# Query tiles of consecutive rows, sines in one run and paired scale factors in a fused attention and convolution kernel

## The chip, the cores and the metric

The kernel runs on one core of one Trainium2 chip. The metric is the time of one execution on the device in microseconds (us); quoted times are medians, with the lowest and highest in brackets. Engines: PE multiplies matrices (PEld is its weight load), DVE is the vector engine, ACT the scalar engine, POOL issues most loads, SP issues stores. In these traces the instructions of an engine start in the order in which they were compiled, and a ready one behind a waiting one waits with it, so the compiled order on each engine matters. Times inside a run are counted from the start of its span; line numbers with an L are those of the kernel named, and the changed kernel's differ from the kernel before.

## The reference, cut to what matters

Eight batches, eight heads, 576 rows, 64 columns per head. Attention with random features is followed by a gated convolution along the rows.

```python
h = x @ omega.T - ...;  phi = exp(h - max(h)) / sqrt(m)      # features of q and k
kv = einsum('bhsm,bhsd->bhmd', phi(k), v);  z = sum(phi(k))
num, den = phi(q) @ kv, phi(q) @ z
x = (num / (den + 1e-06)).transpose(0, 2, 1, 3).reshape(B, S, H * D)
x1, x2, x3 = split(x @ w_proj)
y = x1 * irfft(rfft(x2) * rfft(filter)) * x3
out = y @ w_out
```

## The kernel before

Two generators are woven into one stream of instructions: `attention()` works on pairs of batches, `hyena()` does the projections and the convolution of the pair before. Each `yield` says how much of the work it just put out weighs, and the weaver takes turns by these weights.

A query tile holds, in each partition, four consecutive rows of every head (packets of 512 B in the load):

```python
t_ = nat.tile([P, H, NT, D], BF16, name=f"{which}n", bufs=2)
nc.gpsimd.dma_start(
    out=t_[:, hs].rearrange("p h t d -> p h (t d)"),
    in_=src[b, hs, 0:SM, :].rearrange("h (p t) d -> p h (t d)", t=NT))
```

The values are scaled by one factor per row of each head, which one broadcast element carries:

```python
vc = att.tile([P, H, NT, D + 1], BF16, name="vc", bufs=2)
...
nc.vector.tensor_tensor(out=vc[:, :, :, 0:D], in0=vn[:],
    in1=vc[:, :, :, D : D + 1].to_broadcast([P, H, NT, D]), op=ALU.mult)
```

The output of a batch is normalised into four tiles `xb`, then turned back behind all four, with a permutation and a strided write:

```python
for t in range(NT):
    ps = two_banks()
    for h in range(H): ...                     # 8 matmuls with kv
    xbs.append(normalise(ps))
    yield 3 * U
for cb in range(CB):
    tp = bank()
    for t in (3, 0, 1, 2):
        nc.tensor.matmul(out=tp[:].rearrange("p (c t) -> p t c", t=NT)[:, t],
                         lhsT=xbs[t][:, cb, :], rhs=perm[:], start=True, stop=True)
    nc.scalar.copy(out=xt[:, :, cb, :], in_=tp[:].rearrange("p (g c) -> p g c", g=4))
    yield U
```

The loads stand at the head of the program: keys, values and queries of batch 0, the three thirds of `wproj`, keys, queries and values of batch 1, left-over queries, `wout`, keys and queries of batch 2, then the filter. `load_filter()` also puts out seven additions and subtractions on DVE, the "folds", as soon as the weave reaches it. Sines for the transform tables are computed in three runs on ACT with exponentials between them.

The softmax here doesn't subtract the row's maximum and nothing guards it: scores larger than these inputs give would overflow.

Of the kernel before, what the change touches and what calls it, by code (L numbers as in the profile page):

```python
# [18 lines left out]
P = 128  # L19
# [23 lines left out]
def kernel(  # L43
# [14 lines left out]
    DM = 512  # L58
# [30 lines left out]
    def load_main(b, which, parts=1, between=None):  # L89
        src = {"q": q, "k": k, "v": v}[which]  # L90
        t_ = nat.tile([P, H, NT, D], BF16, name=f"{which}n", bufs=2)
        step = H // parts
        for h0 in range(0, H, step):
            hs = slice(h0, h0 + step)
            nc.gpsimd.dma_start(
                out=t_[:, hs].rearrange("p h t d -> p h (t d)"),
                in_=src[b, hs, 0:SM, :].rearrange("h (p t) d -> p h (t d)", t=NT),
            )
            if between is not None and h0 == 0:
                between()  # L100
        nat_tiles[which, b] = t_
# [27 lines left out]
    load_main(0, "q", 2)  # L129

    wproj = const.tile([P, CB, 3 * DM], BF16, name="wproj")
    for g in (1, 0, 2):
        cs = slice(g * DM, (g + 1) * DM)
        nc.gpsimd.dma_start(
            out=wproj[:, :, cs], in_=moe_w_proj[:, cs].rearrange("(c p) n -> p c n", p=P)
        )
    for w in "kqv":
        load_main(1, w)
# [12 lines left out]
    for j in range(2):  # L151
# [5 lines left out]
    perm = const.tile([P, P], BF16, name="perm")  # L157
    id48 = ident[:, 0:96].rearrange("p (j q) -> p j q", j=2)
    nc.vector.tensor_copy(
        out=perm[:, 0:64].rearrange("p (j q) -> p j q", j=2), in_=id48[:, :, 0:32]  # L160
    )
    nc.vector.tensor_copy(out=perm[:, 64:96], in_=ident[:, 96:128])
    nc.vector.tensor_copy(
        out=perm[:, 96:128].rearrange("p (j q) -> p j q", j=2), in_=id48[:, :, 32:48]
    )


# [3 lines left out]
    for j in range(NV):  # L171
        t_ = const.tile([P, 2, H, D + 1], BF16, name=f"vcl{j}")
        nc.vector.memset(t_[:], 0.0)
        vcl_buf.append(t_)
# [26 lines left out]
    def sines():  # L201
# [48 lines left out]
        def sine(bias, o, x):  # L250
            nc.scalar.activation(out=o, in_=x, func=AF.Sin, scale=-two_pi / S, bias=bias)

        def periodic(bias, o, r_):

            sine(
                bias,
                o[:, 0 : 3 * P].rearrange("p (j c) -> p j c", j=3),
                r_[:, 0:P].unsqueeze(1).to_broadcast([P, 3, P]),
            )
            sine(  # L260
                bias,
                o[:, 3 * P : S].rearrange("p (j s) -> p j s", j=3),
                r_[:, P : P + SL].unsqueeze(1).to_broadcast([P, 3, SL]),
            )


        gn = hy.tile([P, S], BF16, name="x2", bufs=2)
        for n, pieces in (
# [29 lines left out]
            if c == 0:  # L298
                sine(ph[:, 2:3], gtab[:, 0, :], ra)
                sine(zb[:], gtab[:, 1, :], r)  # L300
            elif c == 1:
                sine(ph[:, 0:1], gtab[:, 2, :], ra)
            else:
                periodic(ph[:, 1:2], gtab[:, 3], ra[:, 0:192])
                periodic(ph[:, 0:1], gn[:], ra[:, 192:384])
        for j in range(2):
            ts(out=gns[:, j], in0=gn[:], scalar1=mk[:, j : j + 1], scalar2=None, op0=ALU.mult)
        nc.vector.memset(fwar[:], 0.0)

# [37 lines left out]
    sines()  # L347
# [7 lines left out]
    def load_filter():  # L355
        ff = hy.tile([P, 4, DM], BF16, name="x13", bufs=3)
        fg = hy.tile([P, 4, DM], BF16, name="x13", bufs=3)
        fh = hy.tile([P, 4, DM], BF16, name="x13", bufs=3)
        fsrc = moe_filter_fft.rearrange("(j s) n -> s j n", j=3)
        nc.gpsimd.dma_start(out=ff[:, 0:3], in_=fsrc[0:P])  # L360
        for j in range(2):
            rows = slice(j * SL, (j + 1) * SL)
            nc.gpsimd.dma_start(out=fg[rows, 0], in_=fsrc[P:192, j])
            nc.gpsimd.dma_start(out=fg[rows, 1], in_=fsrc[P:192, 2])
            nc.gpsimd.dma_start(out=fh[rows, 0:3], in_=fsrc[P:192])
        for x, o, y, z, op in (
            (ff, 3, 0, 1, ALU.add),
            (ff, 3, 3, 2, ALU.add),
            (ff, 0, 0, 2, ALU.subtract),
            (ff, 1, 1, 2, ALU.subtract),  # L370
            (fg, 0, 0, 1, ALU.subtract),
            (fh, 0, 0, 1, ALU.add),
            (fh, 0, 0, 2, ALU.add),
        ):
            nc.vector.tensor_tensor(out=x[:, o], in0=x[:, y], in1=x[:, z], op=op)
        filt["b"] = [ff[:, 0], ff[:, 1], fg[:, 0]]
        filt["a"] = [ff[:, 3], fh[:, 0]]
# [56 lines left out]
    def max_to_c(c_out, ekf, n):  # L434
# [13 lines left out]
        with nc.allow_low_precision(reason="a bf16 factor of both sums"):  # L448
            for o, part in c_out:
                m_ = mx[part, 0:n]  # L450
                if n > H:
                    m_ = m_.rearrange("p (h t) -> p h t", h=H)
                nc.vector.reciprocal(out=o, in_=m_)
# [15 lines left out]
    def normalise(ps):  # L469
# [4 lines left out]
        xb = att.tile([P, CB, P], BF16, name="xb", bufs=4)  # L474
# [8 lines left out]
        return xb  # L483

    def attention():
        U = 1.0 / 90.0
        for i in range(B // 2):
# [5 lines left out]
            for bb in range(2):  # L493
# [5 lines left out]

                kt = att.tile([P, H, 2, P], BF16, name="kt", bufs=1)  # L500
                qt = att.tile([P, H, 2, P], BF16, name="qt", bufs=1)

                def turn(dst, src, g):
                    transposes(
                        dst[:, 4 * g : 4 * g + 4, :, :].rearrange("p h u c -> p (h u) c"),
                        [
                            src[:, h, 2 * u2 : 2 * u2 + 2, :].rearrange("p t d -> p (t d)")
                            for h in range(4 * g, 4 * g + 4)
                            for u2 in range(2)
                        ],  # L510
# [12 lines left out]
                for g in range(2):  # L523
                    turn(kt, kn, g)
                    yield 3 * U
                    for h in (4 * g, 4 * g + 2):
                        key_features(
                            ek[:, h : h + 2, :, :].rearrange("p h t m -> p (h t m)"),
                            [kt[:, hh, u2, :] for hh in (h, h + 1) for u2 in range(2)],
                        )  # L530
                        yield 3 * U
                if bb == 0:
# [12 lines left out]
                        [(vcl[hs, j, :, D], hs) for j, hs in enumerate(halves)], ekl[:], H  # L545
                    )
                    for j, hs in enumerate(halves):
                        nc.vector.tensor_tensor(
                            out=vcl[hs, j, :, 0:D],
                            in0=vl[hs, :, :],  # L550
                            in1=vcl[hs, j, :, D : D + 1].to_broadcast([SL, H, D]),
                            op=ALU.mult,
                        )
                    yield U
                for g in range(2):
                    turn(qt, qn, g)
                    yield 3 * U

                if bb == 1:
# [18 lines left out]
                vc = att.tile([P, H, NT, D + 1], BF16, name="vc", bufs=2)  # L578
                max_to_c(
                    [(vc[:, :, :, D], slice(0, P))],  # L580
# [3 lines left out]
                nc.vector.tensor_tensor(  # L584
                    out=vc[:, :, :, 0:D],
                    in0=vn[:],
                    in1=vc[:, :, :, D : D + 1].to_broadcast([P, H, NT, D]),
                    op=ALU.mult,
                )

                eqt = att.tile([P, NPAIR, 2, 2, 2, P], BF16, name="eqt", bufs=1)
                for pr in range(NPAIR):
                    ps = two_banks()
                    for j in range(2):
# [3 lines left out]
                            rhs=qt[:, 2 * pr : 2 * pr + 2, :, :],  # L598
# [3 lines left out]
                    nc.scalar.activation(  # L602
                        out=eqt[:, pr].rearrange("p j h u c -> p j (h u c)"), in_=ps[:], func=AF.Exp
                    )
                    yield 3 * U

                ps = two_banks()
                for h in range(H):
                    o = ps[:, h // 4, (h % 4) * (D + 1) : (h % 4 + 1) * (D + 1)]
                    nc.tensor.matmul(  # L610
                        out=o, lhsT=ekl[:, h, :], rhs=vcl[:, bb, h, :], start=True, stop=False
                    )
                    for t in range(NT):
# [3 lines left out]
                            rhs=vc[:, h, t, :],  # L617
# [13 lines left out]
                for t in range(NT):  # L631
                    ps = two_banks()
                    for h in range(H):
                        nc.tensor.matmul(
                            out=ps[:, h // 4, (h % 4) * (D + 1) : (h % 4 + 1) * (D + 1)],
                            lhsT=eqt[:, h // 2, t % 2, h % 2, t // 2, :],
# [6 lines left out]

                for cb in range(CB):
                    tp = bank()
                    for t in (3, 0, 1, 2):
                        nc.tensor.matmul(  # L647
                            out=tp[:].rearrange("p (c t) -> p t c", t=NT)[:, t],
                            lhsT=xbs[t][:, cb, :],
                            rhs=perm[:],  # L650
                            start=True,
                            stop=True,
                        )
                    nc.scalar.copy(  # L654
                        out=xt[:, :, cb, :], in_=tp[:].rearrange("p (g c) -> p g c", g=4)
                    )
                    yield U
# [13 lines left out]
            tp = bank()  # L671
            for cb in range(CB):
                nc.tensor.matmul(
                    out=tp[:, cb * P : (cb + 1) * P],
                    lhsT=xb[:, cb, :],
                    rhs=ident[:],
                    start=True,
                    stop=True,
                )
            nc.scalar.copy(out=xtl[:], in_=tp[:].rearrange("p (c j s) -> p j c s", c=CB, j=2))  # L680
# [275 lines left out]
```

## Time and profile before

| | before |
|---|---|
| time, us | 365.05 (364.85 to 365.65), 3 runs |
| span of the profiled run, us | 363.8 |
| busy PE, DVE, ACT, POOL, us | 303.5, 227.8, 198.2, 47.5 |
| values of batch 0 / 1 scaled at | 41.3 / 64.2 |
| left-over product x13l of pair 0 / 1 / 2 / 3 at | 140.8 / 233.5 / 291.8 / 341.3 |

`vc` of a batch is the last thing that kv of that batch needs; x13l ends the projections of a pair of batches; xt, used further down, is a batch's output after the turn back. From x13l of pair 0 to that of pair 2 two pairs pass in the settled part of the kernel; I call these 150.9 us the steady stretch. The lines of the profile are in the prediction.

### The profile page before, as it was taken

Reading aid. Unit: us, or ns where it says so; the run is one execution under the profiler, and the core shown is the slowest. Engines: PE = TensorE matmul, PEld = TensorE weight load, DVE = VectorE, ACT = ScalarE, POOL = GpSimd, SP = SyncE. Lnnn points to the kernel's source line nnn. Section 1 sums busy time; section 2 is a strip of 40 time slices with the busy share of each in tenths; the row PEclk is TensorE's granted clock in tenths of the full one; section 3 lists DMA queues with packets and bytes.
Section 4 is the critical chain, followed back from the end, with each engine's and each line's share of the span. In section 5 each row is a group of like instructions: output and inputs, shape, how many; then the busy total and the mean of one; then the engine's idle time right before and its main releaser. Section 6 shows DMA issues by size and latency. Waiting matters only on the chain.

```text
span 363.8 us, 6044 instructions
## 1 busy us (share of the span) xinstructions
PE 303.5 (83%) x2434; PEld 175.6 (48%) x2434; DVE 227.8 (63%) x460; ACT 198.2 (54%) x302; POOL 47.5 (13%) x70
## 2 busy tenths in 40 slices
PE   1715386897678999988999996999998999988993
PEld 1503373753245557546556545756443544433541
DVE  7438679641976787697289999386069343076440
ACT  2796138089954654733886761664583322763123
POOL 8723352200110100213000000000000000000000
PEclk9966689899586999999999999999999999999998
DMA  8999997921674241789941100003401014220034
GB/s 89 185 202 196 185 136 88 155 28 12 69 114 55 14 53 20 142 108 169 165 54 37 29 0 2 2 17 100 146 23 36 2 59 141 63 58 2 0 117 144
DMA packets 47740, 29.26 MB, mean 80 GB/s; under 512 B 14432, under 2 KB 42080, under 8 KB 47712
## 3 DMA queue, kind: packets, MB, share of 16 engines
q0 software_dynamic: 40912, 17.31, 39.5%
q1 hardware_dynamic: 6800, 11.57, 10.5%
q8 instruction: 19, 0.31, 0.4%
q14 instruction: 9, 0.07, 0.1%
HBM read 34.64 MB, written 9.44 MB: 121 GB/s over the span
## 4 chain that ended last, share of the span: by engine, by line
PE 46%; DVE 23%; DMA 13%; ACT 11%; issue 5%; POOL 1%; POOLq 0%; ACTq 0%; DVEq 0%
PE h L837 9%; PE h L882 7%; PE h L899 7%; PE h L715 6%; DMA x<-in_moe_filter_fft_dram 5%; DMA kn<-in_k_dram 4%; DVE xb L475 4%; PE h L647 3%; DVE vc L584 3%; DMA vn<-in_v_dram 2%; PE a L614 2%; PE h L853 2%; ACT ek L467 2%; DMA qn<-in_q_dram 2%; PE h L878 2%
## 5 line engine op out<-in xcount | busy, mean ns | idle before, releaser
L837 PE MATMUL h<-xt,wproj 128*128 128x512 bf16 x256 | 61.0, 387 | 3.4 <-DVE x L846 3.4
L467 ACT ACTIVATE ek<-a 128x1024 bf16<-128x1024 f32 x32 | 32.4, 1044 | 36.7 <-PE a L460 36.7
L909 ACT COPY osb<-h 128x512 f32<-128x512 f32 x36 | 21.1, 586 | 44.2 <-PE h L899 34.9
L837 PEld LDWEIGHTS <-wproj 128*128 128x128 bf16 x256 | 25.2, 100 | 32.7 <-issue 6.4
L845 ACT CAST x<-h 128x512 bf16<-128x512 f32 x32 | 19.2, 600 | 28.8 <-PE h L837 21.9
L602 ACT ACTIVATE eqt<-a 128x1024 bf16<-128x1024 f32 x32 | 32.2, 1065 | 4.2 <-PE a L595 4.1
L889 DVE TENSOR_TENSOR yt<-x,h 128x512 bf16<-128x512 bf16 x32 | 21.9, 684 | 18.3 <-PE h L882 18.3
L846 DVE TENSOR_TENSOR x<-h,x 128x512 bf16<-128x512 f32 x32 | 22.0, 687 | 16.7 <-PE h L837 12.7
L899 PE MATMUL h<-wout,yt 128*128 128x512 bf16 x128 | 31.3, 380 | 0.0
L715 PE MATMUL h<-wproj,xf 128*128 128x512 bf16 x128 | 31.0, 379 | 0.3 <-DVE xf L690 0.2
L654 ACT CAST xt<-h 128x512 bf16<-128x512 f32 x32 | 17.4, 593 | 21.7 <-PE h L647 21.6
L475 DVE TENSOR_TENSOR xb<-a,rden 128x512 bf16<-128x512 f32 x36 | 24.0, 681 | 3.9 <-PE h L647 3.6
L882 PE MATMUL h<-gtab,xs 128*128 128x64 bf16 (+1 forms) x128 | 26.1, 286 | 0.0
L460 PE MATMUL a<-om,kt 128*128 128x256 bf16 x128 | 22.3, 304 | 3.9 <-DVE kt L432 3.1
L595 PE MATMUL a<-qt,om 128*128 128x512 bf16 x64 | 20.9, 417 | 5.3 <-ACT eqt L602 2.4
L788 PE MATMUL h<-x,fwb 128*128 128x512 bf16 x72 | 20.9, 419 | 4.1 <-ACT sw L772 2.7
L882 PE MATMUL h<-gtab,sp 128*128 128x64 bf16 (+1 forms) x128 | 24.1, 286 | 0.0
L432 DVE COPY kt<-t 128x1024 bf16<-128x1024 bf16 x16 | 11.0, 685 | 17.8 <-PE t L431 14.3
L722 ACT CAST x<-h 128x512 bf16<-128x512 f32 x32 | 19.2, 616 | 5.2 <-PE h L715 5.2
L614 PE MATMUL a<-vc,ek 128*128 128x65 bf16 x256 | 12.8, 205 | 9.4 <-DVE vc L584 9.4
L431 PE MATMUL t<-ident,kn 128*128 128x128 bf16 x128 | 12.1, 247 | 8.7 <-DMA kn<-in_k_dram 7.1
L715 PEld LDWEIGHTS <-xf 128*128 128x128 bf16 x128 | 12.3, 98 | 13.6 <-DVE xf L690 0.8
(190 smaller groups left out, 557.9 us busy)
## 6 DMA issues: line engine op xcount, KB each, us to landing
out_dram<-osb SPq DMA_DIRECT2D x24, 256.0 KB, 2.0
vn<-in_v_dram POOLq DMA_DIRECT2D x8, 512.0 KB, 6.9
kn<-in_k_dram POOLq DMA_DIRECT2D x7, 512.0 KB, 6.2
qn<-in_q_dram POOLq DMA_DIRECT2D x7, 512.0 KB, 7.7
out_dram<-osb SPq DMA_DIRECT2D x24, 128.0 KB, 2.4
sw<-sp SPq DMA_DIRECT2D x16, 128.0 KB, 2.3
wproj<-in_moe_w_proj_dram POOLq DMA_DIRECT2D x3, 512.0 KB, 12.3
kn<-in_k_dram POOLq DMA_DIRECT2D x2, 256.0 KB, 4.6
```

Source lines behind the costliest of these rows:

```text
L460: nc.tensor.matmul(out=pf[:, g * 256 : (g + 1) * 256], lhsT=kt, rhs=om2[:].rearrange("p j m -> p (j m)"), start=True, stop=True,)
L467: nc.scalar.activation(out=ek_out, in_=pf, func=AF.Exp)
L475: nc.vector.tensor_tensor(out=xb[:].rearrange("p c (g d) -> p (c g) d", d=D).rearrange("p (a h) d -> p a h d", a=2), in0=psh[:, :, :, 0:D] ...
L595: nc.tensor.matmul(out=ps[:, j, :], lhsT=om2[:, j, :], rhs=qt[:, 2 * pr : 2 * pr + 2, :, :], start=True, stop=True,)
L602: nc.scalar.activation(out=eqt[:, pr].rearrange("p j h u c -> p j (h u c)"), in_=ps[:], func=AF.Exp)
L715: nc.tensor.matmul(out=p2[:], lhsT=lhs[:, ct, :], rhs=wproj[:, ct, DM : 2 * DM], start=(ct == 0), stop=(ct == CB - 1),)
L837: nc.tensor.matmul(out=pp[:], lhsT=wproj[:, ct, off + nb * P : off + (nb + 1) * P], rhs=xt[:, :, ct, :], start=(ct == 0), stop=(ct == CB - 1),
L846: nc.vector.tensor_tensor(out=x13[:, nb, :], in0=p3[:], in1=x1[:], op=ALU.mult)
L882: nc.tensor.matmul(out=dst, lhsT=xs[:, m, ns] if m < 2 else sp[:, m - 2, ns], rhs=gtab[:, m, cs], start=False, stop=(m == 3),)
L889: nc.vector.tensor_tensor(out=yt[:, nb, :], in0=x13s[bb][:, nb, :], in1=o2[:], op=ALU.mult)
L899: nc.tensor.matmul(out=po[:], lhsT=yt[:, nb, t * P : (t + 1) * P] if t < NT else ytl[:, nb, :, :].rearrange("p b s -> p (b s)"), rhs=wout[ ...
L909: nc.scalar.copy(out=osb[:], in_=po[:])
```

## The change

The intent: with query tiles of consecutive rows the output comes out in natural row order, so plain transposes turn it back; the sines run together and change the ACT table less often; each scale factor is stored twice, side by side, so that DVE reads pairs. The order of the first loads changes too, the filter goes into other buffers, and a turn back now follows each second normalised tile instead of all four.

```diff
+        if which == "q":
+            t_ = nat.tile([P, NT, H, D], BF16, name="qn", bufs=2)
+            src = q[b].rearrange("h (j s) d -> s j h d", j=3)
+            for j in range(3):
+                nc.gpsimd.dma_start(out=t_[:, j], in_=src[0:P, j])
+            for j in range(2):
+                nc.gpsimd.dma_start(out=t_[j * SL : (j + 1) * SL, 3], in_=src[P:192, j])
 ... loads
-    load_main(0, "q", 2)
+    load_main(0, "q")
+    load_main(1, "k")
-    for g in (1, 0, 2): ... wproj third g
-    for w in "kqv":
-        load_main(1, w)
+    load_wproj(1)
+    load_main(1, "v")
+    load_main(1, "q")
+    load_wproj(0)
+    load_wproj(2)
 ... sines: make_residues() at the start, and behind the exponentials of batch 0
+                if b == 0:
+                    with tc.issue_after(last.ins):
+                        last_sine = sines()
 ... key features of batch 1 held behind the last sine
+                        with tc.issue_after(last_sine) if b == 1 else nullcontext(): ...
 ... filter
-        ff = hy.tile([P, 4, DM], BF16, name="x13", bufs=3)
-        fg = hy.tile([P, 4, DM], BF16, name="x13", bufs=3)
+        ff = hy.tile([P, 4, DM], BF16, name="yt", bufs=2)
+        fg = hy.tile([P, 4, DM], BF16, name="yt", bufs=2)
 ... values: factors twice, in a tile of D + 2
+        nc.vector.tensor_tensor(
+            out=vc_[:, :, 0:D].rearrange("p n (d e) -> p n d e", e=2),
+            in0=v_.rearrange("p n (d e) -> p n d e", e=2),
+            in1=vc_[:, :, D : D + 2].unsqueeze(2).to_broadcast([np_, n, D // 2, 2]),
+            op=ALU.mult)
 ... turn back, inside the loop over t; xb has 3 buffers instead of 4
-                for cb in range(CB): ... permuting matmuls, copy, yield U
+                    if t % 2 == 1:
+                        turn_back(xt[:, t - 1 : t + 1].rearrange("p g c x -> p (g c) x"), xbs)
+                        xbs = []
+                        yield 2 * U
```

## The prediction

> **What bounds the kernel now.** I read the page's slices first, then the chain that ended last in order of time, then busy time by stretch, then the groups by shape, and last the timeline where those pointed.
>
> ```profile
> PE   1715386897678999988999996999998999988993
> DVE  7438679641976787697289999386069343076440
> DMA  8999997921674241789941100003401014220034
> ```
>
> One slice is 9.1 us. PE is full from about slice 12 on. Before that it is often idle, most in slices 0 to 4, exactly where the DMA engines are at 9. So there are two regimes: a start that the loads pace, and a long part that PE paces.
>
> ```profile
> 20.00:30.00 10.00, 2.79 (x18) 1.72 (x17) 3.01 (x7) 7.95 (x11) 3.21 (x4) 0.51 1.39 200
> 30.00:45.00 15.00, 6.83 (x65) 4.66 (x63) 12.00 (x25) 5.95 (x8) 4.54 (x8) 0.64 1.37 193
> 200.00:240.00 40.00, 37.06 (x326) 22.47 (x325) 33.14 (x65) 23.36 (x34) 0.00 (x0) 1.00 0.03 7
> ```
>
> These are the busy times by stretch (length, then PE, weight loads, DVE, ACT, POOL, granted clock, DMA share, GB/s). From 20 to 45 us PE works 9.6 of 25 us at about half clock, while the loads run at 193 to 200 GB/s. From 200 to 240 us PE works 93% at full clock.
>
> ```profile
> 5.47 8.11 DMA vn<-in_v_dram
> 13.86 13.54 DMA kn<-in_k_dram
> 27.68 16.80 DMA x<-in_moe_filter_fft_dram
> ...
> 61.93 2.31 DVE vc L584
> ```
>
> The chain (start, length, what) is three loads in a row up to 44.5 us. The third is the filter, which nobody needs before the filter transform, far later. It is on the chain because of DVE's fixed order:
>
> ```profile
> 44.51 1.22 DVE L375 TENSOR_TENSOR x<-x 128x512 bf16<-128x512 bf16 x3 [2.62 <-DMA x<-in_moe_filter_fft_dram]
> 45.64 0.69 DVE L622 CAST kv<-a 128x520 bf16<-128x520 f32 x1
> ```
>
> The filter's folds stand in front of the copy of kv of batch 0. PE had finished kv at about 43.5 us; everything of batch 0 behind it, its xt (52 to 54 us) and batch 1's value scaling (61.9 to 64.2 us), queues after the filter.
>
> Why do the loads chain? At each pause POOL waits for the load eight issues before: the 13th (kn, at 13.86 us) for the 5th (vn), the 21st (filter, 27.68 us) for the 13th. So eight loads are in flight, served in order. From the packet records of the saturated stretch I take the service rates: 386 packets of 512 B per us, 203 of 1024 B, and some 1040 of 128 B.
>
> ```profile
> L584 DVE TENSOR_TENSOR vc<-vn,vc 128x2048 bf16<-128x2048 bf16 x8 | 18.3, 2292 | 0.2
> L437 DVE TENSOR_TENSOR h<-ek 128x2048 bf16<-128x2048 bf16 x8 | 9.8, 1224 | 10.4 <-ACT ek L467 10.3
> L614 PE MATMUL a<-vc,ek 128*128 128x65 bf16 x256 | 12.8, 205 | 9.4 <-DVE vc L584 9.4
> L647 PE MATMUL h<-perm,xb 128*128 128x128 bf16 x128 | 17.8, 315 | 1.1 <-DVE xb L475 1.1
> ```
>
> ```profile
> 224.81 0.62 PE L431 MATMUL t<-ident,qn 128*128 128x128 bf16 x8 [0.26 <-DVE qt L432]
> ...
> 226.81 1.48 PE L647 MATMUL h<-perm,xb 128*128 128x128 bf16 x12 [0.22 <-DVE xb L475]
> ```
>
> Groups (busy, mean ns, idle before), then, from the timeline, two rows at full clock. Scaling the values takes 2292 ns where another two-operand instruction of the same size and type takes 1224, and PE waits 9.4 us for it in all. The turn back of the output (L647) is slower than a plain transpose: take off one matmul's latency (0.31 and 0.22 us) and the pitch is 1.17/11 = 106 ns against 0.40/7 = 57 ns.
>
> **What the Trainium skill says.** *VectorE: DVE Perf Modes*, section "Side-by-side: where the cycles go for N=2048 bf16", gives 2293 ns at one element per cycle and 1224 ns at two. The trace agrees: 2292 and 1224 ns in the rows above. *Vector Engine (DVE) Microarchitecture Reference*, section 5.1, says the two-per-cycle mode needs every operand 2 bytes wide, with innermost step 1 and more than one element there; one element reread as an operand ran at one per cycle, while rows of two qualify. That explains L584 now (step 0) and promises 1224 ns for pairs of equal factors; no run yet shows it. *DMA: Bandwidth & Descriptors*, section "Specifications", wants at least 512 B for line rate. The trace agrees in direction: 128 B packets move 133 GB/s of destination bytes, 512 B packets 198. *ScalarE: Activation LUTs*, "What ACT_TABLE_LOAD costs", says about 1283 ns per load plus a drain. The trace has seven loads of 1283 ns.
>
> **The change, part by part.**
>
> *Values.* 8 scalings x (2292 - 1224) = 8.5 us less DVE, plus 8 halves x (689 - 420, the time of a 512-element two-operand group) = 2.2 us. DVE is not the bound; what counts is PE's wait for vc. Of 9.4 us, 6.8 lie between 30 and 65 us, inside the start; 2.6 us in three waits come after 130 us. I count 2 us.
>
> *Turn back.* The permuting matmul writes PSUM at a stride of four; now 128 plain bf16 transposes write densely. 128 x 49 ns = 6.3 us of PE. A quarter lies in batches 0 and 1, where PE is not the bound; the other 96 give 4.7 us, on the engine that paces. ACT's copies go from four of 512 (a group of four took 2.05 us) to two of 1024 (about 1.04 us each, as the exponentials): even.
>
> *Sines.* 7 table loads become 3, 4 x 1.28 = 5.1 us of ACT. They lie in the start, where ACT has slack (5.95 of 15 us busy). Alone worth nearly nothing.
>
> *Query loads.* A query tile becomes five DMAs with 4096 packets of 128 B instead of 1024 of 512 B: 4096/1040 = 3.94 us of service instead of 2.65, so +1.3 us each; POOL's issue grows from 0.87 to about 4 us (three of 0.88, two of 0.69, by the rows of equal packet counts). After the start each query tile has about a batch of lead, so I count 1 us in all.
>
> *Order of the start.* This is the largest term, and partly the scheduler's: in the compiled order of the changed kernel DVE's filter folds stand after all of batch 0's attention and just around batch 1's value scaling. Batch 0 no longer waits for the filter, but the filter comes later. In flight order, from 12 us (end of vl's data): q0 3.94, k1 2.65, one wproj third 2.52, v1 2.65, q1 3.94, two thirds 5.04, left queries 0.98, wout 2.52, k2 2.65, q2 3.94, v2 2.65, first filter piece 1.9: data complete at 47.4, plus about 2 us to land. The same sum for the kernel before gives 42.9 where the trace shows 44.5, so I add 1.6: the first piece lands at 51, the other pieces (640 packets of 1024 B, 3.2 us) by 54.2. Batch 0: queries land at 18, both transposes copied at 23 (4 us of DVE work stands between them), exponentials to 28, sines to 33.5, vc about 29, xt at 37 instead of 54. Then DVE's queue stops at the folds. Batch 1's vc can end at about 55.4 instead of 64.2, when the second-last filter piece has come and its own 1.22 us have run: 8.8 us won. Behind it PE (13.65 of the next 15 us) and then ACT (19.4 of 20 from 80 to 100 us) are busy and keep the lead.
>
> Sum: 8.8 + 4.7 + 2 - 1 = 14.5; 365 - 14.5 = 350.5. I say 350.
>
> **Rivals.**
> 1. *The filter still sets the start, and lands later than my sum* because small query DMAs occupy five of eight slots and starve the engines between landings. For: the eight-slot waits are there. Against: five query pieces plus three others still hold over 5 us of service in flight, more than the 2 us of landing. If so, vc of batch 1 comes at 60 and the kernel at 355.
> 2. *The start's gain is given back*: from 80 to 100 us ACT is full, and the granted clock was 0.80 and 0.77 in 80 to 120 us; if ACT's work there cannot move forward, or the clock drops longer, only 4 us of the start survive: 355 to 357.
> 3. *More comes*: batch 0's hyena work, done before the filter lands, fills PE early, so that 12 us or more are won in the start, and denser transposes let PE close some of its remaining 18 us of idle time after 120 us: 343 to 346.
> 4. *Query loads become the wait*: 4 us of POOL issue before each value load. PE's waits for qn after the start are absent in the trace before. If they appear, +3 us.
>
> **Range and chances.** The turn back and the values are durations that the trace already shows for the same shapes: 6 to 7 us, little doubt. The start spreads from 4 to 13 us. So 342 to 358 holds eight in ten. Within 2% means above 357.7, so faster 0.88, same 0.11, slower 0.01.
>
> **What would show it.** vc scaling at about 1224 ns. Turn back transposes at a pitch near 57 ns and 6 us less PE time. Three table loads. Query packets of 128 B. xt of batch 0 near 37 us; the first filter fold near 51 us with DVE idle before it; batch 1's vc ending near 55 us. PE waits for vc after 130 us gone. It is wrong if the folds start past 57 us, if PE waits for queries, or if a stretch between 80 and 120 us is as long as the lead it was given.

## The result, and the profile after

The changed kernel took 351.85 us (351.25 to 353.25, 3 runs) against 365.05. The ratio is 0.9642, with a 95% interval of 0.9594 to 0.969. A ratio here is the mean time of one kernel's runs over that of the other's in the same rounds, so not quite the ratio of the medians.

The busy shares in 40 slices (tenths; now 8.75 us each) of the changed kernel:

```profile
PE   2755667985969999989889969999998999989993
DVE  7787298517687796961689975854287431185530
DMA  8999999937692408994941000022420034120035
```

PE starts earlier: slices 1 to 4 read 7, 5, 5, 6 where they read 7, 1, 5, 3. The same shows by stretch (length, then PE, weight loads, DVE, ACT, POOL, granted clock, DMA share, GB/s):

```profile
20.00:30.00 10.00, 6.49 (x51) 4.04 (x52) 8.62 (x14) 6.08 (x7) 5.20 (x7) 1.00 1.71 186
30.00:45.00 15.00, 9.05 (x117) 7.78 (x114) 6.51 (x17) 8.15 (x11) 7.86 (x13) 0.66 1.65 188
200.00:240.00 40.00, 35.84 (x415) 23.84 (x413) 27.34 (x51) 19.36 (x26) 0.00 (x0) 0.96 0.09 27
```

From 20 to 45 us PE now does 15.5 us of work instead of 9.6, with loads at 186 to 188 GB/s instead of 193 to 200. But from 200 to 240 us it does less, 35.84 against 37.06 us, at a granted clock of 0.96 instead of 1.00. Other work stands in this window, since the kernel is 14 us ahead, so this is only a first sign that the later part did not deliver.

The chain that ended last, in order of time (start, length, what):

```profile
15.09 10.29 DMA vn<-in_v_dram
...
26.81 9.00 DMA ql<-in_q_dram
...
38.84 10.12 DMA yt<-in_moe_filter_fft_dram
...
52.73 1.23 DVE vc L472
```

The filter is still in it, but what it holds is batch 1 and not batch 0 any more. DVE's timeline shows where the folds (L389) stand:

```profile
28.18 1.22 DVE L472 TENSOR_TENSOR vc<-vn,vc 128x2048 bf16<-128x2048 bf16 x1
...
30.87 0.70 DVE L668 CAST kv<-a 128x520 bf16<-128x520 f32 x1 [0.88 <-PE a L660]
...
49.12 0.42 DVE L389 TENSOR_TENSOR yt<-yt 128x512 bf16<-128x512 bf16 x1
...
52.73 1.22 DVE L472 TENSOR_TENSOR vc<-vn,vc 128x2048 bf16<-128x2048 bf16 x1
```

kv of batch 0 is copied at 30.9 instead of 45.6 us, and the folds lie between the steps of batch 1's maximum. The groups that the change touched (busy, mean ns, idle before):

```profile
L515 PE MATMUL h<-ident,xb 128*128 128x128 bf16 x144 | 12.8, 235 | 4.0 <-DVE xb L499 3.7
L660 PE MATMUL a<-vc,ek 128*128 128x65 bf16 x256 | 12.5, 203 | 6.2 <-DVE vc L472 6.2
L472 DVE TENSOR_TENSOR vc<-vn,vc 128x2048 bf16<-128x2048 bf16 x8 | 9.7, 1216 | 0.1
```

Scaling takes 1216 ns instead of 2292. PE waits 3.7 us for xb in front of the turn back, which was 1.1 us. Milestones of both kernels:

| us from the start of the span | before | after | lead |
|---|---|---|---|
| vc of batch 0 | 41.3 | 29.4 | 11.9 |
| xt of batch 0 complete | 54.1 | 43.3 | 10.8 |
| vc of batch 1 | 64.2 | 53.9 | 10.3 |
| filtered left-over rows (xr) of pair 0 | 97.8 | 87.8 | 10.0 |
| x13l of pair 0 | 140.8 | 126.6 | 14.2 |
| x13l of pair 1 | 233.5 | 219.0 | 14.5 |
| x13l of pair 2 | 291.8 | 278.0 | 13.8 |
| end | 363.8 | 350.1 | 13.7 |

So the start gave 10 us, the stretch to x13l of pair 0 another 4, and the almost two thirds of the kernel after it nothing. The prediction had 8.8 us in the start and most of the rest spread over the whole. The steady stretch even grew from 150.9 to 151.4 us.

### The profile page after: what moved, and what is told of

Read it like the earlier page. It is cut to its first block, busy times and chain, and to the rows that moved or that the text cites. A ratio compares the mean times of both kernels' runs of the same rounds, so it can differ in the third digit from the quotient of the medians.

```text
span 350.1 us, 6058 instructions
## 1 busy us (share of the span) xinstructions
PE 295.5 (84%) x2434; PEld 169.4 (48%) x2434; DVE 218.3 (62%) x457; ACT 192.2 (55%) x282; POOL 72.0 (21%) x101
## 3 DMA queue, kind: packets, MB, share of 16 engines
q0 software_dynamic: 65984, 17.31, 50.3%
## 4 chain that ended last, share of the span: by engine, by line
PE 45%; DVE 21%; DMA 13%; ACT 13%; issue 5%; POOL 2%; ACTq 0%; POOLq 0%; DVEq 0%
PE h L863 9%; PE h L908 7%; PE h L925 6%; PE h L741 6%; DMA vn<-in_v_dram 5%; DMA ql<-in_q_dram 3%; DMA yt<-in_moe_filter_fft_dram 3%; PE h L515 3%; DVE xb L499 2%; DMA out_dram<-osb 2%; PE h L879 2%; ACT ek L491 2%; PE a L660 2%; PE h L904 2%; DVE h L451 2%
## 5 line engine op out<-in xcount | busy, mean ns | idle before, releaser
L863 PE MATMUL h<-xt,wproj 128*128 128x512 bf16 x256 | 59.4, 380 | 3.5 <-DVE x L872 3.4
L519 ACT COPY xt<-h 128x1024 bf16<-128x1024 bf16 x16 | 16.2, 1012 | 45.4 <-PE h L515 45.4
L644 ACT ACTIVATE eqt<-a 128x1024 bf16<-128x1024 f32 x32 | 31.1, 1032 | 9.7 <-PE a L637 9.4
L871 ACT CAST x<-h 128x512 bf16<-128x512 f32 x32 | 18.8, 592 | 26.0 <-PE h L863 20.2
L96 POOL DMA_DIRECT2D qn<-in_q_dram x24 | 21.2, 900 | 22.2 <-PE t L445 21.7
L484 PE MATMUL a<-om,kt 128*128 128x256 bf16 x128 | 21.2, 300 | 3.0 <-DVE kt L446 2.3
L748 ACT CAST x<-h 128x512 bf16<-128x512 f32 x32 | 18.7, 599 | 7.4 <-PE h L741 6.8
L741 PEld LDWEIGHTS <-xf 128*128 128x128 bf16 x128 | 12.2, 97 | 13.4 <-DVE xf L716 0.2
L925 PEld LDWEIGHTS <-yt 128*128 128x128 bf16 x128 | 11.5, 98 | 13.2 <-DVE yt L915 2.3
```

The source lines that it names most:

```text
L96: nc.gpsimd.dma_start(out=t_[:, j], in_=src[0:P, j])
L484: nc.tensor.matmul(out=pf[:, g * 256 : (g + 1) * 256], lhsT=kt, rhs=om2[:].rearrange("p j m -> p (j m)"), start=True, stop=True,)
L644: last = nc.scalar.activation(out=eqt[:, pr].rearrange("p j t c -> p j (t c)"), in_=ps[:], func=AF.Exp)
L741: nc.tensor.matmul(out=p2[:], lhsT=lhs[:, ct, :], rhs=wproj[:, ct, DM : 2 * DM], start=(ct == 0), stop=(ct == CB - 1),)
L863: nc.tensor.matmul(out=pp[:], lhsT=wproj[:, ct, off + nb * P : off + (nb + 1) * P], rhs=xt[:, :, ct, :], start=(ct == 0), stop=(ct == CB - 1),
L925: nc.tensor.matmul(out=po[:], lhsT=yt[:, nb, t * P : (t + 1) * P] if t < NT else ytl[:, nb, :, :].rearrange("p b s -> p (b s)"), rhs=wout[ ...
```

## The experiments

Each kernel was timed in rounds with the kernel before on the same chip; in those rounds the kernel before had medians of 364.07, 364.34 and 364.23 us (362.4 to 365.95 over all). All twelve gave correct results. Two questions were open: what in the start gave the 10 us, and why the turn back, whose saving had seemed the surest, gave nothing. The expectations name their theories by letters; beside each I say in words what was at stake. Milestones come from one profiled run of each kernel; how far they repeat can be seen in the last column, where kernels with the same turn back and scaling agree within 0.5 us. A warning for all: every edit moves the compiled order on the engines, so "one part alone" is never only that part. I read in each trace what order came out.

| kernel | time, us | ratio to before, 95% | vc of batch 1 | x13l of pair 0 | steady stretch |
|---|---|---|---|---|---|
| before (first profile) | 365.05 | | 64.2 | 140.8 | 150.9 |
| after | 351.85 | 0.9642 [0.9594, 0.969] | 53.9 | 126.6 | 151.4 |
| b_folds_late | 361.64 (360.7 to 361.96) | 0.9934 [0.9886, 0.9981] | 61.6 | 136.9 | 150.9 |
| b_order | 363.58 (362.67 to 365.49) | 0.9998 [0.9943, 1.0053] | 63.7 | 139.2 | 150.9 |
| b_values | 360.13 (358.96 to 360.91) | 0.9896 [0.9837, 0.9956] | 63.1 | 137.6 | 148.4 |
| b_sines | 362.36 (361.55 to 363.31) | 0.9959 [0.991, 1.0008] | 62.9 | 138.5 | 151.0 |
| b_order_folds | 355.21 (354.31 to 356.52) | 0.9753 [0.9698, 0.9808] | 55.2 | 131.3 | 151.4 |
| b_queries | 359.5 (358.16 to 360.5) | 0.9877 [0.9825, 0.9928] | 58.7 | 132.9 | 153.8 |
| b_packets | 360.84 (360.38 to 361.68) | 0.9916 [0.9885, 0.9947] | 59.5 | 136.1 | 151.0 |
| a_no_queries | 357.0 (356.19 to 357.72) | 0.9803 [0.9747, 0.9859] | 59.7 | 135.5 | 148.4 |
| a_no_order | 349.56 (348.7 to 350.88) | 0.9609 [0.9559, 0.9659] | 51.8 | 123.8 | 151.0 |
| n_late_turn | 339.21 (339.09 to 339.92) | 0.9323 [0.9295, 0.9351] | 51.3 | 119.1 | 146.3 |
| n_folds_last | 347.47 (346.81 to 349.41) | 0.9535 [0.9502, 0.9568] | 49.1 | 124.1 | 151.5 |
| n_both | 339.45 (339.37 to 340.77) | 0.9334 [0.9303, 0.9365] | 48.6 | 119.2 | 146.3 |

Names that begin with b are the kernel before with one part added, with a the changed kernel with one part taken back, with n new versions.

### The start

**b_folds_late.** The kernel before, with the seven folds held behind the last normalised tile of batch 0. The prediction's main cause by itself.

```diff
-        for x, o, y, z, op in ( ... ):
-            nc.vector.tensor_tensor(out=x[:, o], in0=x[:, y], in1=x[:, z], op=op)
+        with tc.issue_after(marks[0]):      # last normalise of batch 0
+            for x, o, y, z, op in folds:
+                nc.vector.tensor_tensor(out=x[:, o], in0=x[:, y], in1=x[:, z], op=op)
```

> The kernel before with one thing moved: DVE's seven filter folds are put behind the last normalise of batch 0 (issue order only). Theory A, the prediction's: in the kernel before the folds in front of batch 0's copy of kv hold the whole start, so moving them wins a large part of the 10 us by which batch 1's vc came earlier: 357 to 361 us. Theory B: the start was held by the load of batch 1's keys (landed at 27.4 us, with PE and DVE queued behind its transposes for 6 to 7 us) and by the DVE work that then came in one lump; the folds cost only the 2.6 us that DVE sat idle in front of them: 362.5 to 365 us.

Ratio 0.9934. The kv copy of batch 0 ends at 44.0 instead of 46.3 us, vc of batch 1 at 61.6 instead of 64.2. So the folds in front of kv were a real stop, but worth only 2.6 us: vc of batch 0 itself is not ready before 40.9 us, because the keys of batch 1 (copied at 28.1 and 30.0 us, after DVE had idled 7.4 us in front of them) stand in front of batch 0's maximum and scaling. DVE's timeline:

```profile
28.10 0.69 DVE L436 COPY kt<-t 128x1024 bf16<-128x1024 bf16 x1 [7.40 <-PE t L435]
...
38.59 2.29 DVE L592 TENSOR_TENSOR vc<-vn,vc 128x2048 bf16<-128x2048 bf16 x1
```

Another stop lies in front of the one that I had named.

**b_order.** The kernel before, with the loads in the order of the change.

```diff
     load_main(0, "q", 2)
+    load_main(1, "k")
-    for g in (1, 0, 2): ... wproj third g
-    for w in "kqv":
-        load_main(1, w)
+    load_wproj(1)
+    load_main(1, "v")
+    load_main(1, "q")
+    load_wproj(0)
+    load_wproj(2)
```

> The kernel before with the load order of the change alone: keys of batch 1 ahead of the projection weights, one third of the weights, then values and queries of batch 1, then the other two thirds. The same bytes are in flight in front of the filter, so theory A expects within 1 us of before (364 to 366). Theory B expects batch 1's keys to land near 20 us instead of 27.4, the 6 us PE wait for them to vanish, and 357 to 361 us.

Ratio 0.9998, nothing. DVE's timeline of this kernel tells why:

```profile
43.59 0.42 DVE L381 TENSOR_TENSOR x<-x 128x512 bf16<-128x512 bf16 x1 [7.37 <-DMA x<-in_moe_filter_fft_dram]
43.93 0.69 DVE L628 CAST kv<-a 128x520 bf16<-128x520 f32 x1
...
61.36 2.29 DVE L590 TENSOR_TENSOR vc<-vn,vc 128x2048 bf16<-128x2048 bf16 x1
```

The keys of batch 1 come early (copied by 23.2 us) and vc of batch 0 is ready at 34.5 instead of 41.3 us. Then DVE stands 7.37 us at the first fold, with the kv copy behind it. Of the 6.8 us won at the first stop, 0.6 us are left when xt of batch 0 is complete (53.5 us).

**b_order_folds.** Both: the load order, and the folds held behind the first step of batch 1's maximum.

```diff
+ the load order of b_order
+        with tc.issue_after(marks[0]):      # first maximum of batch 1
+            for x, o, y, z, op in folds: ...
```

> The kernel before with the load order of the change and with the filter folds put behind the first maximum of batch 1, both together. Apart they gave 0 and 0.7%: with the load order batch 0's value scaling ended 6.8 us earlier, but the folds then held batch 0's copy of kv until 44.6 us; with the folds moved behind batch 0, its scaling still ended at 40.9 us. Theory C: the late keys and the folds are two stops one behind the other, each hiding what the other costs, so together they win clearly more than the sum: batch 1's vc at 54 to 58 us instead of 64.2, and 355 to 359 us. Theory A or B alone, or a third stop: vc of batch 1 stays after 60 us and the time at 361 to 364.

Ratio 0.9753, where the two parts alone gave 0.9934 and 0.9998. DVE's timeline:

```profile
36.08 0.70 DVE L635 CAST kv<-a 128x520 bf16<-128x520 f32 x1 [0.62 <-PE a L627]
...
49.49 0.42 DVE L385 TENSOR_TENSOR x<-x 128x512 bf16<-128x512 bf16 x1
...
52.90 2.28 DVE L597 TENSOR_TENSOR vc<-vn,vc 128x2048 bf16<-128x2048 bf16 x1
```

kv at 36.1 us, the folds around batch 1's scaling, vc of batch 1 at 55.2 us: 9.0 us of the change's 10.3, without touching queries, sines or values. Two stops in series: taking away either gives little (0.66% and 0.02%), taking away both gives 2.5%. The folds stand a little further back here than in b_folds_late, but in both they are behind batch 0's kv.

**b_sines.** The kernel before, with the sines in one run and the filter in the buffers named yt.

```diff
-    sines()
+    make_residues()
 ... behind the exponentials of batch 0
+                if b == 0:
+                    with tc.issue_after(last.ins):
+                        last_sine = sines()
 ... key features of batch 1 held behind the last sine; ff, fg from "yt" (bufs 2) instead of "x13" (bufs 3)
```

> The kernel before with the sines in one run alone (with the filter's two tiles in the buffers that this frees, as in the change). Three table loads instead of seven. The prediction: ACT has slack there, so next to nothing, 364 to 365.5. Theory B allows more, because batch 0's query features no longer wait for the third group of sines (they ended at 37.4 us before, at 27.8 us in the changed kernel): 361 to 364.

Ratio 0.9959, and the interval contains 1. The query features of batch 0 are ready at 23.5 us instead of 37.4 and kv is copied at 36.9 us. But DVE stands 5.42 us at the first fold at 45.6 us, now in front of batch 0's outputs: xt comes at 53.0 us, as before (54.1). Again a first stop was taken away and a second kept the time. That saved table loads are "alone worth nearly nothing" held; that they stand in front of the query features of batch 0 I had not seen.

**a_no_order.** The changed kernel, with the load order of before.

```diff
     load_main(0, "q")
-    load_main(1, "k")
-    load_wproj(1)
-    load_main(1, "v")
-    load_main(1, "q")
-    load_wproj(0)
-    load_wproj(2)
+    for g in (1, 0, 2):
+        load_wproj(g)
+    for w in "kqv":
+        load_main(1, w)
```

> The changed kernel with the load order as before. The folds stay late in the compiled order. Theory A: nothing lost, 351 to 353. Theory C: batch 1's keys land 5 to 7 us later, in front of PE and DVE, and most of that is lost: 355 to 359.

349.56 us: faster than the changed kernel, by the ratios 0.9609 against 0.9642 (the intervals overlap). This refutes the theory, for which I had expected 355 to 359 us, that the late keys of batch 1 were the second stop because they land late. They land late here too, and it costs nothing:

```profile
25.77 1.22 DVE L470 TENSOR_TENSOR vc<-vn,vc 128x2048 bf16<-128x2048 bf16 x1
...
29.06 0.69 DVE L444 COPY kt<-t 128x1024 bf16<-128x1024 bf16 x1 [2.07 <-PE t L443]
31.21 0.70 DVE L666 CAST kv<-a 128x520 bf16<-128x520 f32 x1 [1.45 <-PE a L658]
```

The copy of batch 1's keys waits at 29 us, but vc of batch 0 stands in front of it and is done. In b_folds_late the copy of the same keys, at 28.1 us and after a wait of 7.4 us, stood in front of vc. So a late landing is no cost by itself; it costs where batch 0's work stands behind the copy. There are two ways out of that stop. One is to load the keys early (b_order; the changed kernel too copies them before vc, at 25.0 and 27.6 us, after waits of 0.86 and 0.26 us). The other is a compiled order with batch 0's work in front, as here, and it follows from other parts: the sines alone (b_sines) and the query tiles alone (b_queries, below) each bring vc of batch 0 to about 34 us. Beside these the new load order adds nothing. With it xt of batch 0 even comes later (43.3 against 39.0 us), since PE waits 2.3 us for left-over queries and 2.4 us for keys of batch 2 in front of the two turn backs.

**n_folds_last.** a_no_order with the folds behind the kv copy of batch 1, to see what the remaining stop is worth.

```diff
+ the load order of a_no_order
+        with tc.issue_after(marks[1]):      # kv copy of batch 1
+            for x, o, y, z, op in folds: ...
```

> The same 349.6 us version with the filter folds put behind batch 1's copy of kv (issue order on DVE only). If DVE's place in front of batch 1's value scaling is still what the filter costs, batch 1's vc ends at 45 to 48 us instead of 51.8 and the whole at 345 to 347. If the keys of batch 2, or something else in front of it, hold it as well, vc ends after 50 and the time stays at 349 to 350.

347.47 us, just above what the first theory had. vc of batch 1 comes 2.7 us earlier than in a_no_order (49.1 us), but x13l of pair 0 is at 124.1 against 123.8 us. The lead is gone by then. The trace records the stretches in which PE was granted half its clock. These records (outside the run's end) add up to 41.0 us here and 34.1 us in a_no_order, which is part of it; I did not look for the rest.

### The steady stretch

Here 150.9 us pass in the kernel before. From the trace I split them into time in which a PE instruction ran and idle time, by the instruction that followed.

| | steady stretch | PE works | PE idle |
|---|---|---|---|
| before | 150.9 | 141.4 | 9.6 |
| b_values, and the same in a_no_queries | 148.4 | 141.1 | 7.2 |
| b_queries | 153.8 | 140.5 | 13.2 |
| after | 151.4 | 139.2 | 12.2 |
| n_late_turn | 146.3 | 137.8 | 8.5 |

**b_values.** The kernel before, with the factors in pairs.

```diff
-                vc = att.tile([P, H, NT, D + 1], BF16, name="vc", bufs=2)
+                vc = att.tile([P, H, NT, D + 2], BF16, name="vc", bufs=2)
 ... scaling as in the change
```

> The kernel before with pairs of equal scale factors alone. The scaling of the values takes about 1215 ns instead of 2292. The prediction: 2 us from the waits after 130 us, and at most a little more from the two waits in the start (one of 4.6, one of 2.2 us): 361 to 363. Rival: DVE is ahead of what paces everywhere and the waits close up elsewhere: 364.5 to 365.5.

Ratio 0.9896; the 360.13 us lie below both expectations. The steady stretch is 2.5 us shorter, of which 2.1 are PE's wait for vc. DVE is busy 9.4 us less over the kernel, so most of that was beside other work, as predicted. The rest of the gain is in the start; the half-clock records there add up to 27.3 us instead of 44.4, which is part of it, and I did not separate it further.

**b_queries.** The kernel before, with the query tiles and the plain turn back after each second tile.

```diff
+        if which == "q": ... five loads of a tile [P, NT, H, D]
-        xb = att.tile([P, CB, P], BF16, name="xb", bufs=4)
+        xb = att.tile([P, CB, P], BF16, name="xb", bufs=3)
-                for cb in range(CB): ... permuting matmuls, copy, yield U
+                    if t % 2 == 1:
+                        turn_back(xt[:, t - 1 : t + 1].rearrange("p g c x -> p (g c) x"), xbs)
+                        xbs = []
+                        yield 2 * U
```

> The kernel before with the query tiles of consecutive rows and the plain turn back alone. The prediction's terms: turn back 4.7 us less PE on the pacing part, query loads 1 us more, so 361 to 362 from these. If the turn back's saving is given back in waits for xb, as the trace of the changed kernel suggests (PE waited 2.8 us in front of turn backs after 120 us, and the lead did not grow after the 127th us): 363 to 365 unless the start moves too. The compiled order has the folds behind batch 0's copy of kv here, which by theory C may win about 2 us in the start.

Ratio 0.9877, faster than expected, but by two opposite parts. The start gains 7.9 us up to x13l of pair 0. The compiled order now has the folds behind batch 0's kv, and most of batch 0's maximum in front of the copies of batch 1's keys (29.4 and 33.9 us). The steady stretch loses 2.9 us. The turn back itself is cheaper by 3.3 us (8.2 us of permuting matmuls gone, 4.9 us of transposes in their place), close to the 3.1 us that 64 times 49 ns make. But PE idles 2.8 us more in front of the turn back, 1.9 us more in front of the transposes of keys, and some of its work runs at half clock.

**a_no_queries.** The changed kernel, with query loads and turn back as before.

```diff
-            t_ = nat.tile([P, NT, H, D], BF16, name="qn", bufs=2) ... five loads
-    load_main(0, "q")
+    load_main(0, "q", 2)
-                    if t % 2 == 1: turn_back(...)
+                for cb in range(CB): ... permuting matmuls, copy, yield U
```

> The changed kernel with query tiles, loads and turn back as before. If the turn back and the loads are worth their own terms alone, 351.9 + 4 = 355 to 356. In the compiled order the folds stand in front of batch 0's x and batch 1's value scaling once more; by theory C that costs most of the start's gain too: 358 to 361.

357.0 us, 5 us slower than the changed kernel and between the two expectations. More than all of that is in the start (vc of batch 1 at 59.7 us, x13l of pair 0 8.9 us later). The steady stretch is 148.4 us, the same as with the values alone. So in both surroundings the new query tiles with their turn back make this stretch about 3 us longer, and the values make it 2.5 us shorter: the two parts add up.

**b_packets.** The kernel before, with each query tile loaded by four DMAs with rows of 128 B. This doubles the suspected cost of the loads without the new turn back.

```diff
+            if which == "q":
+                for t0 in range(NT):
+                    nc.gpsimd.dma_start(
+                        out=t_[:, hs, t0, :],
+                        in_=src[b, hs, 0:SM, :].rearrange("h (p t) d -> p h t d", t=NT)[:, :, t0])
+                continue
```

> The kernel before with nothing changed but its query loads, cut in four DMAs with rows of 128 B in place of 512 B. In the stretch from batch pair 0's left-over product to batch pair 2's (150.9 us before), the small packets cost nothing if they have a batch of lead: 150.4 to 151.5. If they are what costs the query tiles their 3 us there, 153 to 154. In the start the filter lands some 4 us later by the packet count, but the compiled order has the folds behind batch 0's copy of kv, so the total may go either way: 362 to 367.

Queue 0 carried 65856 packets instead of 40912, nearly as many as in the changed kernel (65984). The steady stretch stayed at 151.0 us, with the same 141.4 us of work and 9.6 us idle. The small packets cost nothing there. The whole kernel came out faster than expected (0.9916), all of it before x13l of pair 0. The trace points to order again: batch 0's maximum fell in front of the keys' copies (vc of batch 0 at 32.3 us) and the folds behind the kv copy.

**n_late_turn.** a_no_order, with both turn backs behind the fourth normalised tile as before, and four buffers for xb.

```diff
+ the load order of a_no_order
-        xb = att.tile([P, CB, P], BF16, name="xb", bufs=3)
+        xb = att.tile([P, CB, P], BF16, name="xb", bufs=4)
-                    if t % 2 == 1:
-                        turn_back(xt[:, t - 1 : t + 1].rearrange("p g c x -> p (g c) x"), xbs)
-                        xbs = []
-                        yield 2 * U
+                for t in (1, 3):
+                    turn_back(
+                        xt[:, t - 1 : t + 1].rearrange("p g c x -> p (g c) x"), xbs[t - 1 : t + 1])
+                    yield 2 * U
```

> The changed kernel with the load order of before (the 349.6 us version) and both turn backs of a batch put after its fourth normalise instead of one after each pair (four xb buffers for that). In the stretch from batch pair 0's left-over product to batch pair 2's, the turn back by pairs saves 3.3 us of PE work and adds 3.0 us of waiting for xb in front of the turn backs. If the early place of the turn back is the cause, these waits fall below 1.5 us and that stretch gets 1.5 to 3 us shorter than 151.0: 347 to 348.5 us. If DVE simply delivers xb late wherever the turn back stands, nothing changes: 349 to 350.

339.21 us (339.09 to 339.92), ratio 0.9323: it beats both kernels, by far more than I expected. The gain over a_no_order is 1.8 us in the start (to xt of batch 1), 2.9 us from there up to x13l of pair 0 and 4.7 us in the steady stretch. And it is not where I looked for it. PE's waits in front of the turn back are unchanged (from 140 to 300 us 2.4 us, against 2.3 in a_no_order). What went are the wait for vc (2.9 to 0.9 us), the wait for query transposes (1.1 to 0.3 us) and 1.6 us of PE's own time. PE's timeline at the vc of batch 6 shows it, first in the kernel before:

```profile
212.88 5.09 PE L837 MATMUL h<-xt,wproj 128*128 128x512 bf16 x22
217.80 0.61 PE L431 MATMUL t<-ident,kn 128*128 128x128 bf16 x8
219.80 0.29 PE L614 MATMUL a<-vc,ek 128*128 128x65 bf16 x4 [1.39 <-DVE vc L584]
```

Then in the changed kernel:

```profile
200.60 0.81 PE L863 MATMUL h<-xt,wproj 128*128 128x512 bf16 x3
201.24 0.61 PE L445 MATMUL t<-ident,kn 128*128 128x128 bf16 x8
201.97 1.02 PE L863 MATMUL h<-xt,wproj 128*128 128x512 bf16 x4
205.44 0.38 PE L660 MATMUL a<-vc,ek 128*128 128x65 bf16 x4 [2.45 <-DVE vc L472]
```

And with the late turn back:

```profile
189.66 1.24 PE L862 MATMUL h<-xt,wproj 128*128 128x512 bf16 x5
190.74 0.39 PE L443 MATMUL t<-ident,kn 128*128 128x128 bf16 x4
191.03 2.75 PE L862 MATMUL h<-xt,wproj 128*128 128x512 bf16 x12
193.61 0.39 PE L443 MATMUL t<-ident,kn 128*128 128x128 bf16 x4
194.25 0.29 PE L658 MATMUL a<-vc,ek 128*128 128x65 bf16 x4 [0.26 <-DVE vc L470]
```

While DVE computes vc (maximum and scaling), PE needs other work in its queue. The kernel before had 22 projection matmuls there, the changed one has 7, the late one 17. So although vc itself got 1.1 us cheaper, PE waits longer for it: 2.45 instead of 1.39 us. The turn backs and their `yield` inside the loop had moved the projection matmuls elsewhere. b_queries and a_no_order have the same 3 and 4 matmuls there, and stops of 2.06 us (for a key copy) and 1.16 us (b_queries) and 2.46 us (a_no_order); a_no_queries and b_values have no stop there. Against these two, which scale the values in the same way and have a steady stretch of 148.4 us, n_late_turn is 2.1 us shorter: at its old place the cheaper turn back gives two thirds of the 3.1 us that its price promises. The fourth xb buffer is not what helped: DVE waited 0.4 us in all in front of its normalising instructions with three buffers and with four.

There is a second cost at the same place. The first vc matmuls take 0.38 us per four in the changed kernel and 0.29 in the other two. In the changed kernel a record of 3.4 us at half clock begins at 204.9 us, 1.9 us after PE fell idle; a_no_order and n_folds_last have one at the same stop, b_queries has 6.8 us. Neither the kernel before nor b_values, a_no_queries, n_late_turn or n_both has any in the steady stretch. The matmuls behind the stop and the eight key transposes after them, which run in that record, take 3.1 us in the changed kernel and 1.8 us before. The page *TensorE: Matmul & The Clock Gate* of the Trainium skill, section "Why this matters for your kernels", says to leave no PE gap above about 3 us between bursts, or the clock falls to half. The traces agree that the clock can fall in a stop, but here one of 2.45 us, with 0.6 us of transposes and seven matmuls in front of it, was enough. Nor does the length of one stop decide it: in the kernel before, a record of 10.2 us at half clock begins inside a stop of 1.43 us (from 90.9 us), while the stops of 1.39 us at 218.4 us and 1.71 us at 277.8 us have none.

What is not settled: I did not hold the number of projection matmuls fixed and move the turn back alone, so how much of the 4.7 us is filler and how much is the clock, and why a_no_order also lost time between 64 and 124 us, is read from traces and was not tested by itself.

**n_both.** n_late_turn with the folds of n_folds_last.

```diff
+ the edits of n_late_turn
+        with tc.issue_after(marks[1]):      # kv copy of batch 1
+            for x, o, y, z, op in folds: ...
```

> Late turn back and late folds together on the 349.6 us version, to see whether they add: 343 to 346 if both theories hold, 347 to 350 if neither does.

339.45 us, the same as n_late_turn. vc of batch 1 is 2.7 us earlier, x13l of pair 0 at 119.2 against 119.1 us. The folds' place has no more to give.

## Why the prediction was right or wrong

The total was right: 350 predicted, 351.85 measured, inside the range. That it came so near is in good part luck. In the sum, the values and most of the start were right; the turn back was to give 4.7 us and the new query tiles lengthened the steady stretch by 3 instead, and what made up for this was not in the sum: 1.5 us more in the start and 4.2 us between 98 and 141 us.

- **Values, 2 us.** Right in mechanism and about in size: 2.5 us of the steady stretch, 1216 ns per scaling against the 1224 promised. But the check "waits for vc after 130 us gone" failed in the changed kernel: there are two, 2.9 us in all. One of 0.48 us is left with the values alone too (b_values), the other of 2.45 us comes with the turn back's order.
- **Start, 8.8 us.** It gave 10.3 us at vc of batch 1, and the estimate of that moment, 55.4 us, was met within 1.5 us (53.9). The mechanism was half right. The folds in front of batch 0 were a stop, but alone worth 0.7% (b_folds_late). A second stood in front of it, the place of batch 1's keys and of the sines in front of batch 0's work; only both removed pay (b_order_folds). The view that the load order was part of the gain was wrong: without it the kernel is not slower (a_no_order). xt of batch 0 came at 43.3 us and not at 37, since PE's queue had two late loads in front of the turn backs; DVE did not idle in front of the first fold, which came at 49.1 us.
- **Turn back, 4.7 us.** This step failed: "the other 96 give 4.7 us, on the engine that paces". The price per transpose was right (a pitch of 57 ns; 3.3 us less PE work in the steady stretch against 3.1 worked out for 64 of them). But I took a saving on the pacing engine for a saving of time. The new tiles with their turn back made the steady stretch about 3 us longer, by waits in front of the turn back, by the projection matmuls that moved away from the wait for vc, and by one stretch at half clock; at the old place (n_late_turn) they shorten it by 2.1. I had looked at how long the new instructions take and not at what stands beside them. The order, in which a turn back follows each second tile, was there to be read before.
- **Query loads, 1 us of loss.** 0 in the steady stretch (b_packets). In the start I did not separate them; PE waited 2.3 us there for left-over queries, a wait of the kind that the prediction had named as a sign of being wrong.
- **Sines, nearly nothing.** Alone 0.4%, with an interval that contains none; but they take part in the first stop. The drain that the prediction names beside each table load does not show: in the kernel before the load of 1.28 us at 14.48 us starts 0.02 us after the end of the exponential in front, and the sine 0.01 us after the load's end.
- **From 98 to 141 us, not in the sum.** 4.2 us were won between the filtered left-over rows and x13l of pair 0. The turn back has 1.1 us less PE time there. The records at half clock that reach into it add up to 13.7 us instead of 17.1, which is up to 1.7 us. The rest is not accounted for.

Of the rivals, the third (more comes) was right in that the start gave 10 and not 8.8 us and the lead reached 14.2 us by x13l of pair 0, but the total did not follow. The filter did not hold the start longer (first), the lead was not given back between 80 and 120 us (second), and PE did not wait for main query tiles after the start (fourth). What happened in place of them, a turn back whose new place took filler away from another wait, was on nobody's list.

## What to carry to other kernels

With engines that run in order, ask of each slow load not when it lands but what stands behind the instruction that waits for it; two such stops in series can each look nearly worthless when removed alone. A saving on the engine that paces is a saving of time only if the order of its queue stays: count the independent instructions that lie between a producer's start and the consumer's wait, before and after. And when one part of a change seems to give nothing, put it in with the order of before: here the same transposes behind the fourth tile turned 351.85 us (349.56 with the old load order) into 339.21.

## What the Trainium skill lacked or had wrong

- *TensorE: Matmul & The Clock Gate*, "Part 4: PE-mode transpose", gives about 275 ns for one transpose in a kernel. Eight in a row took 0.62 us here, a pitch of 57 ns; it is the pitch that one needs for a sum (the page has one for plain matmuls, in another section). That section has no figure for a matmul that writes PSUM at a stride: the permuting one of the kernel before had a pitch of 106 ns.
- The same page, "Why this matters for your kernels", puts the limit for gaps at about 3 us. In the changed kernel 3.4 us at half clock begin 1.9 us into a stop of 2.45 us, and in the kernel before 10.2 us begin inside a stop of 1.43 us, while a stop of 1.71 us has none: the runs give no single length.
- *Vector Engine (DVE) Microarchitecture Reference*, section 5.1, has a row that is read again and again as an operand at two per cycle. The trace agrees for rows of two equal factors: 1216 ns against 2292. What making such pairs costs it does not say: the reciprocal that writes them took 546 ns instead of 358.
- *DMA: Bandwidth & Descriptors*, "Specifications", gives 512 B as the smallest size for line rate; how many smaller packets from HBM are served the page does not say for this chip. Here the loads' trace records give an answer: 128 B packets were served at some 1040 per us (133 GB/s), 512 B packets at 386 per us (198 GB/s). And the quadrupled packet count of the query loads left the steady stretch at 151.0 us (b_packets).
